# Which pairs of the expert layers use products of halves in the second layer

## The chip, the cores and the metric

The kernel runs on one core of a Trainium2 chip: one TensorE (PE, matrix products), VectorE (DVE), ScalarE (ACT), GpSimd (POOL), SyncE (SP, which issues transfers), one on-chip memory of 128 partitions, and PSUM, where PE's products collect. The metric is the device time of one execution in microseconds, the median of several executions.

## The reference

Causal attention with decay, then a dense mixture of four experts over all tokens, then a soft mixture of eight experts with four slots each. The change touches the middle part only:

```python
def _moe_ref(x, domain_probs, w1, w2):
    N, D = x.shape                       # 2304, 512
    E = w1.shape[0]                      # 4 experts, F = 1024
    p = domain_probs / (domain_probs.sum(-1, keepdims=True) + 1e-09)
    out = np.zeros((N, D), dtype=np.float32)
    for e in range(E):
        h = np.maximum(x @ w1[e], 0.0)
        out += p[:, e:e + 1] * (h @ w2[e])
    return out
```

## The kernel before, in words

**Numbers.** Every f32 operand is split into a high and a low f16 part, and each product is the sum of three f16 products: high by high, high by low, low by high. So each logical product of 128x128 weights is three matmuls.

**Tokens.** The 2304 tokens are 18 tiles of 128, six blocks of three tiles (384 columns, `NB`) and three pairs of blocks. Expert 0 runs beside the attention. Experts 1, 2 and 3 follow, pair after pair.

**Products of halves.** For a pair, x is cut in two by tokens and by inner dimension, w1 in two by two, and the four quarter results come from seven products instead of eight (Strassen's scheme in Winograd's form). It needs four sums of quarters of x (`x_sums`, line 696, a chain of 18 steps for one pair on GpSimd, VectorE and ScalarE), sums of quarters of w1, and additions of the products afterwards. There are two versions of the first layer:

- `quad` (matmuls at line 844, sums at 851, high and low parts at 855 and 858): only the first layer goes by halves. The second is `tile_l2`, whole: per tile of 128 tokens 24 matmuls of 128x512 (line 1105) and one weighted sum into the accumulator (line 658).
- `quad_sums` (matmuls 912, sums 929, 934, 987, copies 923, high parts 1400 or 1402, low parts 941 and 998): it also forms sums of quarters of h, because the second layer goes by halves too. That is `outputs`: seven products for each of three tiles, each of 12 matmuls of 128x256 (line 1041), each followed by one or two weighted sums (line 1053). It needs four sums T1 to T4 of quarters of w2 (`w2_sums`, lines 772, 781, 783).

Both versions have the row blocks m = 0 to 3 of a pair's hidden dimension, with seven products of six matmuls of 128x384 each. The operands of the second layer by halves carry the names "11", "12", "22" (quarters of h) and "1" to "4" (sums). `quad_sums` works in temporaries x, y, u and v of 384 columns. Three sets of them are used in turn. PSUM banks are `qA`, `qE`, `qF`.

**Which pair does what.** `PAIRS = (0, 3, 3, 2)` is the number of pairs of each expert by halves in the first layer, `PLAIN = (0, 1, 0, 0)` says that expert 1's pair 0 has a plain first layer (line 1075), and `OUT_H = (0, 0, 3, 2)` how many pairs go by halves in the second layer: none of expert 1, three of expert 2, two of expert 3.

**Memory.** Only one pair's x and sums have a home of their own in experts 2 and 3. All six blocks of x (`x_d`) and the sums of all pairs (`s_d`) are stored to DRAM once and loaded again ahead of each pair (`load_x`). The T sums of expert 3 are also staged in DRAM (`t_d`).

**Weights.** `prep_tasks` prepares an expert's weights: a maximum over the matrix (lines 496, 499, 503), spread over the partitions by a small PE matmul into `mp` (line 448), then a power of two as scale (lines 421 to 451), then high and low parts (541 and 544; 527 and 440 for w2) and sums of quarters (538).

**Order.** A planner, `Sched`, places each task on its engine at build time: a list scheduler with a cost per task and a key as priority, smallest first; some tasks may go to either of two engines. PE's own order is written out by hand (`in_order`). What the planner fixes is the instruction order of each engine; on the chip every engine follows its list and waits on semaphores.

## Time and profile before

| | |
|---|---|
| median of 3 runs | 971.86 us (971.3 to 973.75) |
| profiled execution | 969.51 us |
| its span in the trace | 967.8 us |
| mean granted clock of PE | 0.994 |
| PE busy | 929.4 us, 96% |
| VectorE busy | 674.9 us, 70% |
| ScalarE busy | 492.3 us, 51% |
| GpSimd busy | 423.3 us, 44% |
| chain that ended last | PE 75%, DVE 12%, DMA 3%, ACT 3% |

Busy times of PE overlap at their ends, so the distance between the starts of two runs of matmuls says more than a mean duration. Expert 1's plain layer begins near 357 us, its pair 1 at 417, pair 2 at 477, expert 2 at 535 (pairs 1 and 2 at 593 and 648), expert 3 at 703, and the second expert layer's matmuls at 914.

### The profile page before, as it was taken

Reading aid. Unit: us, or ns where it says so; the run is one execution under the profiler, and the core shown is the slowest. Engines: PE = TensorE matmul, PEld = TensorE weight load, DVE = VectorE, ACT = ScalarE, POOL = GpSimd, SP = SyncE. Lnnn points to the kernel's source line nnn. Section 1 sums busy time; section 2 is a strip of 40 time slices with the busy share of each in tenths; the row PEclk is TensorE's granted clock in tenths of the full one; section 3 lists DMA queues with packets and bytes.
Section 4 is the critical chain, followed back from the end, with each engine's and each line's share of the span. In section 5 each row is a group of like instructions: output and inputs, shape, how many; then the busy total and the mean of one; then the engine's idle time right before and its main releaser. Section 6 shows DMA issues by size and latency. Waiting matters only on the chain.

```text
span 967.8 us, 22183 instructions
## 1 busy us (share of the span) xinstructions
PE 929.4 (96%) x8984; PEld 627.1 (65%) x8984; DVE 674.9 (70%) x1295; ACT 492.3 (51%) x1094; POOL 423.3 (44%) x416
## 2 busy tenths in 40 slices
PE   7988999999999999999999999999999999999995
PEld 3567778787878865455454577686868768655331
DVE  7989987879776489747566687868987485433313
ACT  6878878878687465246143542616453250212123
POOL 3998786785654377731004340726553150000000
PEclk9999999999999999999999999999999999999998
DMA  8889999999999630643311344243433027913795
GB/s 227 187 171 169 187 184 197 195 192 163 202 177 224 120 121 25 258 182 124 111 65 44 123 163 151 76 143 121 164 101 132 1 76 238 348 70 122 239 359 195
DMA packets 270054, 153.50 MB, mean 159 GB/s; under 512 B 231776, under 2 KB 233824, under 8 KB 269952
## 3 DMA queue, kind: packets, MB, share of 16 engines
q1 hardware_dynamic: 269904, 152.02, 61.1%
q8 instruction: 70, 1.15, 0.5%
q14 instruction: 32, 0.26, 0.1%
q10 hardware_dynamic: 48, 0.07, 0.0%
HBM read 94.02 MB, written 16.25 MB: 114 GB/s over the span
## 4 chain that ended last, share of the span: by engine, by line
PE 75%; DVE 12%; DMA 3%; ACT 3%; issue 2%; POOL 2%; SPq 2%; DVEq 0%; ACTq 0%; POOLq 0%
PE pso L1105 10%; PE qA L912 7%; PE pso L612 6%; PE psh L591 6%; PE qA L1041 5%; PE qE L1041 4%; PE qE L912 4%; PE psh L634 3%; PE pso L652 3%; PE qF L1041 3%; PE s L1533 3%; PE qA L844 2%; PE pv L1622 2%; PE pso L1041 2%; PE qF L912 2%
## 5 line engine op out<-in xcount | busy, mean ns | idle before, releaser
L1041 PEld LDWEIGHTS <-arena 128*128 128x128 f16 x1260 | 123.1, 98 | 17.8 <-issue 1.8
L912 PEld LDWEIGHTS <-arena 128*128 128x128 f16 x840 | 82.0, 98 | 55.2 <-issue 3.5
L1402 POOL TENSOR_SCALAR arena<-arena 128x384 f16<-128x384 f32 (+5 forms) x75 | 56.8, 760 | 125.7 <-ACT arena L923 34.4
L591 PE MATMUL psh<-arena 128*128 128x128 f16 x1728 | 101.9, 219 | 0.0
L612 PE MATMUL pso<-arena 128*128 128x512 f16 x432 | 100.2, 382 | 0.0
L591 PEld LDWEIGHTS <-arena 128*128 128x128 f16 x1728 | 97.3, 98 | 0.4
L1105 PE MATMUL pso<-arena 128*128 128x512 f16 x432 | 95.0, 379 | 0.0
L1574 ACT ACTIVATE arena<-s,mx,qs 128x320 f32<-128x320 f32 (+4 forms) x144 | 91.6, 642 | 4.8 <-POOL arena L1591 1.8
L912 PE MATMUL qA<-arena 128*128 128x384 f16 x480 | 87.3, 326 | 0.7 <-DVE arena L929 0.3
L941 POOL TENSOR_TENSOR arena<-arena 128x384 f16<-128x384 f32 x64 | 63.9, 1008 | 46.6 <-ACT arena L1400 45.2
L1400 ACT ACTIVATE arena<-arena 128x384 f16<-128x384 f32 (+5 forms) x119 | 70.7, 605 | 26.8 <-DVE arena L934 18.0
L1591 POOL TENSOR_TENSOR arena<-arena 128x128 f16<-128x128 f32 (+4 forms) x79 | 69.6, 902 | 13.9 <-ACT arena L1400 12.0
L1105 PEld LDWEIGHTS <-arena 128*128 128x128 f16 x432 | 42.3, 98 | 49.8
L1554 DVE TENSOR_REDUCE mx<-s 128x1 f32<-128x576 f32 (+4 forms) x76 | 64.5, 850 | 8.9 <-PE s L1533 8.5
L612 PEld LDWEIGHTS <-arena 128*128 128x128 f16 x432 | 40.5, 99 | 44.1 <-issue 1.6
L1533 PE MATMUL s<-arena 128*128 128x128 f16 (+1 forms) x928 | 65.1, 212 | 4.1 <-ACT arena L1574 3.6
L696 POOL TENSOR_TENSOR arena<-arena 128x768 f32<-128x768 f32 (+2 forms) x25 | 51.4, 2061 | 30.1 <-DVE arena L696 24.8
L538 POOL TENSOR_TENSOR arena<-arena 128x512 f32<-128x512 f32 x23 | 35.1, 1531 | 61.7 <-DVE arena L544 56.4
L1533 PEld LDWEIGHTS <-arena 128*128 128x128 f16 x928 | 57.4, 98 | 6.7 <-issue 5.0
L1041 PE MATMUL qA<-arena 128*128 128x256 f16 x480 | 57.3, 273 | 0.0
L544 DVE SCALAR_TENSOR_TENSOR arena<-arena,wm 128x512 f16<-128x512 f32 x46 | 55.2, 1223 | 2.3 <-ACT arena L541 2.3
L1591 DVE TENSOR_TENSOR arena<-arena 128x64 f16<-128x64 f32 (+4 forms) x69 | 50.3, 767 | 7.1 <-POOL arena L1402 3.7
(275 smaller groups left out, 1860.2 us busy)
## 6 DMA issues: line engine op xcount, KB each, us to landing
arena<-in_moe_w_dram SPq DMA_DIRECT2D x66, 512.0 KB, 4.7
...
arena<-xd SPq DMA_DIRECT2D x10, 768.0 KB, 4.3
arena<-in_moe_w_dram SPq DMA_DIRECT2D x9, 768.0 KB, 9.6
...
xd<-arena SPq DMA_DIRECT2D x6, 768.0 KB, 7.1
...
```

What stands on the lines that cost most here:

```text
L591: nc.tensor.matmul(out=ps[:, m, :], lhsT=wt["w1" + a, 0][:, kk, ms], rhs=xT[j][:, b + kk, ts], start=(n == 0), stop=(n == 3 * KD - 1))
L612: nc.tensor.matmul(out=ops[u], lhsT=a[:, m, ts], rhs=wt["w2" + b, 0][:, m, :], start=(m == 0 and z == 0), stop=(m == KF - 1 and z == 2))
L912: nc.tensor.matmul(out=ps[c], lhsT=wS[e][o][:, w, k, ms], rhs=a[z][:, k], start=(first and i == 0), stop=(i == 5), skip_group_check=True)
L941: h_t[q][m] = y = T(LO, {"DVE": 0.55, "Pool": 1.0}, -30, lambda eng: by[eng].tensor_tensor(out=l_, in0=a, in1=h_, op=ALU.subtract), [y], r ...
L1041: nc.tensor.matmul(out=ps[c, t], lhsT=hq[a][x][:, m, ts], rhs=wq[y][:, m, :], start=(first and m == 0 and n == 0), stop=(m == KF // 2 - 1 ...
L1105: nc.tensor.matmul(out=cell[0], lhsT=a[:, m, ts], rhs=wt["w2" + b, e][:, m, :], start=(len(left) == KF - 1 and z == 0), stop=(not left and ...
L1400: nc.scalar.activation(out=out, in_=x, func=AF.Copy, scale=scale)
L1402: nc.gpsimd.tensor_scalar(out=out, in0=x, scalar1=scale, scalar2=0.0, op0=ALU.mult, op1=ALU.add)
L1533: nc.tensor.matmul(out=o, lhsT=qT[u][:, 2 * h + w, :], rhs=kT[kk][:, 2 * h + w, k0:k0 + n_], start=(w == 0), stop=(w == 1 and mask is None))
L1554: nc.vector.tensor_reduce(out=mx[:, 0:nh].rearrange("p (a h) -> p a h", a=sv.shape[1]), in_=sv, axis=AX.X, op=ALU.max, negate=True)
L1574: nc.scalar.activation(out=P[:, x], in_=sv[:, x // hb, x % hb], func=AF.Exp, scale=qs[u][:, 4:5], bias=mxs[n][:, 4 + x:5 + x], accum_out=s ...
L1591: by[eng].tensor_tensor(out=t[:, :, d0:d0 + n_], in0=P[:, :, s0:s0 + n_], in1=t[:, :, s0:s0 + n_], op=ALU.subtract)
```

## The change

- **Pairs.** `OUT_H` now names pairs: 1 and 2 of expert 1, 0 and 1 of expert 2, 0 and 1 of expert 3. `ORDER` gives the order of pairs: expert 2 begins with pair 2, which goes by halves in the first layer only (`quad` and `tile_l2`), then pairs 0 and 1 in both. Expert 1's pairs 1 and 2 use `quad_sums` and `outputs`.
- **Sums of w2 for expert 1** (`w2_sums(1)`) are new, beside the sums of x; expert 2's follow its w1 preparation; expert 3's T sums stay on the chip, so `t_d`, its stores and its loads are gone.
- **x and its sums.** The home of x is now pair 2's pages (`HOME = 2`). Sums of x are made for pair 1, pair 0, then (behind the sums of w2) pair 2; before it was pair 1, pair 2, pair 0. The pages of blocks 0, 1 and 3 become operands of the second layer ("11", "22", "12") once their x is stored. Expert 1's pair 1 has its own place for "12" (`hq_own`), in the scratch pages of pair 2's sums. `hq_free` makes the writers of those operands wait for stores and sums.
- **Temporaries.** y, u and v have two sets, and x has three places.
- **Scale steps.** The small steps between the maximum and the scale (`A[4]` to `A[6]`) have the key -35 instead of that of their expert. On PE the spread `mp` for expert 1's w2 stands after 24 matmuls of the plain first layer instead of after 72.
- **Weights by operand.** A product waits for its own weights (`w1_of`) and not for all of the matrix.
- **Expert 3's plain last pair** loads one quarter of w1 again, with one ScalarE and one VectorE instruction.
- **End.** Other pages come free at other moments; 89 pages of the second expert layer's weights are loaded ahead of its first matmul, 92 before.

On the whole program PE has 252 more matmuls of 128x256 (1512, 1260 before) and 144 fewer of 128x512 at `tile_l2` (288, 432 before); its other groups keep their counts.

```diff
-OUT_H = (0, 0, 3, 2)
+ORDER = ((), (0, 1, 2), (2, 0, 1), (0, 1))
+OUT_H = ((), (1, 2), (0, 1), (0, 1))
...
+        def w1_of(o):
+
+            if len(w1_t) != 37:
+                return w1_t
+            i = (1, 5, 7, 17, 12, 16, 14)[o]
+            return [w1_t[1 + i], w1_t[19 + i]]
...
-                return in_order(0.98, go, list(deps) + w1_t + s_t[p],
+                return in_order(0.98, go, list(deps) + w1_of(o) + s_t[p],
...
-            x, y, u, v = tmp
+            x = [tmps[0][0], tmps[1][0], third.get((e, p), third[None])][three]
+            y, u, v = tmps[two][1:4]
             X, Y, U = (lambda a=a: a for a in (x, y, u))
-            old, now = free_at[m % len(tmps)], {}
-            free_at[m % len(tmps)] = now
+            wait = hq_free.get((e, p), {})
+            old = {**free_at[two], "4": x_free[three]}
+            free_at[two] = now = {}
...
-        for p in range(PAIRS[e]):
+        for p in ORDER[e]:
             h_t = [{}, {}]
             before = None
-            if p < OUT_H[e]:
+            if p in OUT_H[e]:
...
+    SMALL = -35
...
-        t = T("DVE", 0.1, key, A[4], ta)
-        t = A[5](key, [t])
-        sc_t = T("DVE", 0.5, key, A[6], [t])
+        t = T("DVE", 0.1, SMALL, A[4], ta)
+        t = A[5](SMALL, [t])
+        sc_t = T("DVE", 0.5, SMALL, A[6], [t])
...
-        for p, tmp in ((1, (p_S[0][0], p_S[0][1])), (2, (p_S[0][0], p_S[0][1])), (0, (wA, wA + 2))):
-            x_halves(p, p_S[p])
-            y = y + {1: [], 2: w2_1, 0: e0_t + w1_1}[p]
-            s_t[p] = y = steps(56 + p % 3, x_sums(p, lambda tmp=tmp: [page(x, 2)[:, 0:2 * NB] for x in tmp]), X_COST, y)
+        sums_of_x(1, 56, (p_T[2], p_T[1]), [])
+        sums_of_x(0, 57, (wA + 6, wA + 14), s_t[1] + e0_t + w1_1)
...
+        sums_1, last = w2_sums(1, ams["w2", 1], [raw2 + 2 * i for i in range(4)], w2_end, 57.5, in_place(1, s_t[1] + w1_1))
+        sums_of_x(2, 58, (wA + 6, wA + 14), s_t[0] + last[0])
...
+        for q, p in (("11", xT_page[0]), ("22", xT_page[1]), ("12", xT_page[3]), ("1", hT_p), ("2", hT_p + 3), ("3", wA + 8),
                      ("4", wA + 11)):
...
+        hq_own[1, 1] = {"12": h_of(wA + 4)}
+        hq_free[1, 1] = {"11": kept_x[0], "22": kept_x[1], "12": kept_s[0] + s_t[2]}
+        hq_free[1, 2] = {"12": kept_x[3], "4": kept_x[2]}
...
+        w1_2, last = prep_tasks(2, 0, R, last, [end_s1[-1]], 60, ([p0_, p0_ + 2], [end_s1[0]] + kept_s[1]))
+        last = sums_of_2(last[0:2], (0, 1), 60, w1_2)
```

Three places show how the order moves. In the changed kernel most lines stand 1 to 40 further down: L696 becomes L697, L851 L869, L912 L932, L929 L949, L941 L962, L987 L1012, L1053 L1082, L544 L545, L658 L659, L772 L782.

VectorE where expert 1's pair 1 begins, before (L658 is a tile sum of pair 0's second layer, L696 a step of the sums of x, L851 and L858 are `quad`'s sums and low parts):

```order
L658 SCALAR_TENSOR_TENSOR arena<-pso,pw,arena 128x512
L696 TENSOR_TENSOR arena<-arena 128x768
L658 SCALAR_TENSOR_TENSOR arena<-pso,pw,arena 128x512
L851 TENSOR_TENSOR qF<-qF,arena 128x384
L696 TENSOR_TENSOR arena<-arena 128x768
L858 SCALAR_TENSOR_TENSOR arena<-qF,arena 128x384
L658 SCALAR_TENSOR_TENSOR arena<-pso,pw,arena 128x512
L851 TENSOR_TENSOR arena<-qA,arena 128x384
```

and changed, the same place (L949 and L962 are `quad_sums`' sums and low parts):

```order
L659 SCALAR_TENSOR_TENSOR arena<-pso,pw,arena 128x512
L697 TENSOR_TENSOR arena<-arena 128x768 x4
L659 SCALAR_TENSOR_TENSOR arena<-pso,pw,arena 128x512
L697 TENSOR_TENSOR arena<-arena 128x768 x3
L949 TENSOR_TENSOR qF<-qF,arena 128x384
L697 TENSOR_TENSOR arena<-arena 128x768 x2
L962 TENSOR_TENSOR arena<-arena 128x384
L949 TENSOR_TENSOR arena<-qA,arena 128x384
L659 SCALAR_TENSOR_TENSOR arena<-pso,pw,arena 128x512
```

Before, one step of the sums of x stands behind the pair's first sum `qF`; changed, two stand behind it, seven more with one tile sum between them just ahead, and they belong to pair 2's chain instead of pair 0's.

GpSimd from the end of the weight preparation to expert 1's pairs, before (L538 and L772 are sums of quarters of w1 and w2, L1402 and L941 high and low parts of expert 2's h):

```order
L696 TENSOR_TENSOR arena<-arena 128x768
L538 TENSOR_TENSOR arena<-arena 128x512 x2
L696 TENSOR_TENSOR arena<-arena 128x768 x21
L772 TENSOR_TENSOR arena<-arena 128x2x256 x3
L538 TENSOR_TENSOR arena<-arena 128x512 x8
L1402 TENSOR_SCALAR arena<-arena 128x384 x2
L941 TENSOR_TENSOR arena<-arena 128x384
```

and changed (L1012 is a sum, L1435 a high part of expert 1's h):

```order
L782 TENSOR_TENSOR arena<-arena 128x2x256
L697 TENSOR_TENSOR arena<-arena 128x768
L782 TENSOR_TENSOR arena<-arena 128x2x256 x3
L697 TENSOR_TENSOR arena<-arena 128x768
L782 TENSOR_TENSOR arena<-arena 128x2x256
L697 TENSOR_TENSOR arena<-arena 128x768 x14
L1012 TENSOR_TENSOR arena<-arena 128x384
L1435 TENSOR_SCALAR arena<-arena 128x384
```

Before, the next work of GpSimd behind the sums of x is expert 2's w2 and w1; changed, sums of expert 1's w2 lie between the sums of x, and expert 1's sums of h follow the last fourteen at once.

VectorE at the end of expert 1's pair 2, where expert 2's w1 is prepared, before (L544 is a low part of w1):

```order
L544 SCALAR_TENSOR_TENSOR arena<-arena,wm_6736 128x512 x2
L658 SCALAR_TENSOR_TENSOR arena<-pso,pw,arena 128x512
L544 SCALAR_TENSOR_TENSOR arena<-arena,wm_6736 128x512 x4
L658 SCALAR_TENSOR_TENSOR arena<-pso,pw,arena 128x512
L544 SCALAR_TENSOR_TENSOR arena<-arena,wm_6736 128x512
L929 TENSOR_TENSOR qF<-qF,arena 128x384
L941 TENSOR_TENSOR arena<-arena 128x384
```

and changed (L1082 is an output sum of a product of halves, L869 the first sum of expert 2's `quad`):

```order
L545 SCALAR_TENSOR_TENSOR arena<-arena,wm_6728 128x512 x2
L1082 SCALAR_TENSOR_TENSOR arena<-qF,pw,arena 128x256
L1082 SCALAR_TENSOR_TENSOR arena<-qE,pw,arena 128x256
L545 SCALAR_TENSOR_TENSOR arena<-arena,wm_6728 128x512
L1082 SCALAR_TENSOR_TENSOR arena<-qA,pw,arena 128x256
L545 SCALAR_TENSOR_TENSOR arena<-arena,wm_6728 128x512
L1082 SCALAR_TENSOR_TENSOR arena<-qE,pw,arena 128x256
L545 SCALAR_TENSOR_TENSOR arena<-arena,wm_6728 128x512
L869 TENSOR_TENSOR qF<-qF,arena 128x384
```

Before, the low parts of w1 lie between tile sums of 128x512; changed, between output sums of 128x256, which come more often. Fourteen L545 and fourteen L1082 stand in the stretch whose end is shown.

## Rows read from the trace of the kernel before

**Rows 1.** The page, section 1: engine, busy us (share of the span), instructions.

```profile
PE 929.4 (96%) x8984; PEld 627.1 (65%) x8984; DVE 674.9 (70%) x1295; ACT 492.3 (51%) x1094; POOL 423.3 (44%) x416
```

**Rows 2.** Windows: length, busy us (instructions) by engine, granted clock, DMA share, GB/s.

```profile
380.00:418.00 38.00, 38.00 (x196) 19.06 (x195) 30.65 (x32) 11.46 (x18) 27.50 (x14) 1.00 0.48 190
418.00:477.00 59.00, 58.74 (x315) 30.67 (x313) 35.55 (x59) 27.28 (x49) 7.22 (x5) 1.00 0.42 142
477.00:535.00 58.00, 58.00 (x313) 30.45 (x312) 36.76 (x57) 21.93 (x41) 12.63 (x8) 1.00 0.19 61
535.00:593.00 58.00, 58.00 (x425) 41.53 (x424) 43.90 (x81) 25.29 (x48) 18.29 (x23) 1.00 0.47 151
...
648.00:703.00 55.00, 54.95 (x421) 40.92 (x419) 48.74 (x84) 28.50 (x55) 32.81 (x31) 1.00 0.38 131
920.00:940.00 20.00, 19.40 (x174) 6.36 (x176) 4.32 (x22) 4.89 (x10) 0.00 (x0) 1.00 1.05 397
```

**Rows 3.** PE's waits over the span: total us, times, longest us.

```profile
PE mp L448 <- DVE wm L503: 2.9, 2, 2.2
...
PE qF L1041 <- DVE arena L1053: 0.6, 1, 0.6
...
PE qA L1075 <- DVE arena L1086: 0.2, 1, 0.2
```

**Rows 4.** PE's timeline, expert 1 pair 0's second layer: start us, length, instruction.

```profile
420.32 4.05 PE L1105 MATMUL pso<-arena 128*128 128x512 f16 x18
424.21 1.14 PE L844 MATMUL qA<-arena 128*128 128x384 f16 x6
```

**Rows 5.** PE's timeline, products of an expert 2 pair's second layer.

```profile
640.32 1.47 PE L1041 MATMUL qF<-arena 128*128 128x256 f16 x12
641.63 1.47 PE L1041 MATMUL qE<-arena 128*128 128x256 f16 x12
```

**Rows 6.** VectorE by line and form, 357 to 825: count | busy us, mean ns | idle before.

```profile
L544 DVE SCALAR_TENSOR_TENSOR arena<-arena,wm 128x512 f16<-128x512 f32 x39 | 45.5, 1188 | 0.7 <-ACT arena L541 0.7
L941 DVE TENSOR_TENSOR arena<-arena 128x384 f16<-128x384 f32 x36 | 26.0, 735 | 6.1 <-POOL arena L1402 4.3 <-ACT arena L1400 1.6
L934 DVE SCALAR_TENSOR_TENSOR arena<-qA,arena 128x384 f32<-128x384 f32 x40 | 21.8, 548 | 1.6 <-PE qA L912 1.6
L1053 DVE SCALAR_TENSOR_TENSOR arena<-qA,pw,arena 128x256 f32<-128x256 f32 x40 | 18.8, 475 | 12.6 <-PE qA L1041 12.4
...
L987 DVE TENSOR_TENSOR arena<-arena 128x384 f32<-128x384 f32 x18 | 15.1, 841 | 0.7
...
L658 DVE SCALAR_TENSOR_TENSOR arena<-pso,pw,arena 128x512 f32<-128x512 f32 x18 | 13.4, 747 | 19.5 <-PE pso L1105 19.5
...
L858 DVE SCALAR_TENSOR_TENSOR arena<-qA,arena 128x384 f16<-128x384 f32 x8 | 4.5, 558 | 6.4 <-ACT arena L855 6.3
```

**Rows 7.** GpSimd's timeline, steps of the sums of x.

```profile
387.72 14.41 POOL L696 TENSOR_TENSOR arena<-arena 128x768 f32<-128x768 f32 x7 [1.44 <-DVE arena L696]
```

**Rows 8.** The page, section 6: stores of x, KB each, us from issue to landing.

```profile
xd<-arena SPq DMA_DIRECT2D x6, 768.0 KB, 7.1
```

**Rows 9.** VectorE's timeline while GpSimd works on the sums of x.

```profile
359.38 2.13 DVE L538 TENSOR_TENSOR arena<-arena 128x512 f32<-128x512 f32 x1
361.44 3.44 DVE L544 SCALAR_TENSOR_TENSOR arena<-arena,wm 128x512 f16<-128x512 f32 x2
...
365.73 3.26 DVE L544 SCALAR_TENSOR_TENSOR arena<-arena,wm 128x512 f16<-128x512 f32 x2
```

**Rows 10.** ScalarE's timeline, expert 2 pair 1: writes of the temporary `u`.

```profile
605.13 0.48 ACT L923 ACTIVATE arena<-qF 128x384 f32<-128x384 f32 x1
...
619.01 0.48 ACT L923 ACTIVATE arena<-qF 128x384 f32<-128x384 f32 x1
```

**Rows 11.** VectorE's timeline, the last low part of that pair.

```profile
629.88 1.62 DVE L941 TENSOR_TENSOR arena<-arena 128x384 f16<-128x384 f32 x1
```

**Rows 12.** VectorE's timeline while GpSimd is idle.

```profile
536.21 0.73 DVE L544 SCALAR_TENSOR_TENSOR arena<-arena,wm 128x512 f16<-128x512 f32 x1
```

More of the change, by code (lines that the diff above doesn't have):

```diff
@@ L786, in w2_sums, with halves_tasks @@
                 out[i].append(then(y))
-            last = [ends, ends]
+            last = [ends, ends] if len(all_bufs) < 4 else [*before, *([ends] if c == 0 else [])]
+            done += ends
+        if len(all_bufs) == 4:
+            last = [done, done]
         return out, last
-    carry = []
-    def halves_tasks(e, w1_t, w2_t, s_t, tmps, between=lambda j: [], used_up=None, plain_t=None, next_x=None, t_sums=None,
-                     t_used=None):
+    carry, hq_own, hq_free, prod, third_at = [], {}, {}, {}, {}
+    def halves_tasks(e, w1_t, w2_t, s_t, tmps, between=lambda j: [], used_up=None, plain_t=None, next_x=None, t_sums=None):
         T = sc.task
@@ L1030, in go @@
                 def go():
-                    calm[0] = (e, p, i, t) != (2, 0, 4, TPB - 1)
+                    calm[0] = i < 4 or t < TPB - 1 or (e, then.get((e, p))) not in TENSE
                     if first:
@@ L1219, in halves_tasks, with prep_tasks @@
         return end_s, end, todo
-    def prep_tasks(e, ti, bufs, before, there, key, more=None, mid=None):
+    SMALL = -35
+    def prep_tasks(e, ti, bufs, before, there, key, more=None, mid=None, there_lo=()):
         T = sc.task
@@ L1254, in prep_tasks @@
                     bufs, us = bufs + more[0], (2, 3)
-                    last += [there + more[1]] * 2
+                    last += [more[1]] * 2
                 if n < 4:
@@ L2063, in moe_attention_kernel @@
         kept_s = {p: [T("DMA", 1.0, 90, lambda p=p, i=i: nc.sync.dma_start(out=s_d[p][i], in_=s_place(p, i)), [s_t[p][-1], *s_t[p]])
-                      for i in range(4)] for p in s_t}
-        xR[:] = [xT[0], xT[1], xS[0]]
+                      for i in range(4)] for p in range(len(s_d))}
+        HOME = 2
+        for e, p in ((1, 1), (None, HOME)):
+            xR[(e, p) if e else None] = [xT[2 * p], xT[2 * p + 1], xS[p]]
         def load_x(p, deps, sums=True):
-            out = [T("DMA", 2.0, 30 + x, lambda x=x: nc.sync.dma_start(out=page(xT_page[x], 3), in_=x_d[2 * p + x]),
-                     deps + kept_x[2 * p + x] + kept_x[x] + kept_s[0]) for x in range(2)]
+            out = [T("DMA", 2.0, 30 + x, lambda x=x: nc.sync.dma_start(out=page(xT_page[2 * HOME + x], 3), in_=x_d[2 * p + x]),
+                     deps + kept_x[2 * p + x] + kept_x[2 * HOME + x]) for x in range(2)]
@@ L2071, in load_x, with h_of @@
             if sums:
-                out += [T("DMA", 1.0, 32 + i, lambda i=i: nc.sync.dma_start(out=s_place(0, i), in_=s_d[p][i]), deps + kept_s[p] + kept_s[0])
+                out += [T("DMA", 1.0, 32 + i, lambda i=i: nc.sync.dma_start(out=s_place(HOME, i), in_=s_d[p][i]), deps + kept_s[p])
                         for i in range(4)]
             return out
-        for q, p in (("11", xT_page[3]), ("22", xT_page[4]), ("12", raw2 + 2), ("1", hT_p), ("2", hT_p + 3), ("3", wA + 8),
+        def h_of(p):
+            v = page(p, 3, F16).rearrange("p (z m c) -> p z m c", z=2, c=NB)
+            return [v[:, z] for z in range(2)]
@@ new lines, in moe_attention_kernel, with sums_of_2 @@
+        w2_2, last = prep_tasks(2, 1, R, [last[0], s_t[2]], s_t[2] + kept_s[0], 59,
+                                there_lo=[prod[1, 1, 2, t] for t in range(TPB)] + [third_at[1, 1]])
+        sums_2 = {f"T{i + 1}": [] for i in range(4)}
+        def sums_of_2(last, cs, key, late=[]):
+            y, last = w2_sums(2, ams["w2", 2], R, [w2_2 + x for x in last], key,
+                              in_place(2, [end_s1[0]] + kept_s[1] + kept_x[2] + late), cs)
+            for b, z in named(y).items():
+                sums_2[b] += z
+            return last
@@ L2117, in moe_attention_kernel @@
-        sc.gate = None
-        w2_3, last = prep_tasks(3, 1, R, last, end_1, 60)
-        held_st = {0: [], 1: []}
-        def staged(i, c):
-            x = i // 2
-            v = page(st_pages[x], 1, F16).rearrange("p (z n) -> p z n", z=2)
-            def then(y):
-                y = T("DMA", 0.8, 60, lambda: nc.sync.dma_start(out=t_d[i][:, :, c, :], in_=v), [y])
-                held_st[x] = [y]
-                store_3[i].append(y)
-                return y
-            return (*(v[:, z].rearrange("p (k n) -> p k n", k=2) for z in range(2)),
-                    held_st[x] + [end_s1[-1]] + kept_x[2] + kept_s[2], then)
+            i = ORDER[2].index(p) + 1
@@ L2136, in sums_of_3 @@
-            for x in spent:
-                load_sum(*x)
+            y, last = w2_sums(3, ams["w2", 3], R, [w2_3 + x for x in last], 60.5, in_place(3, end_1))
+            sums_3.update(named(y))
             sc.gate = None
@@ L2349, in used_up @@
         def used_up(p):
+            if p == 0:
+                dyn.free(p0_, 6)
             if p == PAIRS[e] - 1:
-                for x in p_S[0]:
-                    dyn.free(x, 2)
+                dyn.free(raw2, 6)
             fill(0)
@@ L2365, in moe_attention_kernel @@
             dyn.free(p, 3)
-        for x in range(2):
-            xT_page[NBLK - 2 + x], xT[NBLK - 2 + x] = xT_page[x], xT[x]
+        mg = page(dyn.alloc(1))
         side += rest
```

189 lines of the change are left out of this document (103 added, 86 removed).

## The prediction, made before the changed kernel ran

> **What bounds the kernel now.** I read the page first, then the waits of PE, then windows of one token pair each, then PE's and VectorE's timelines at the places the change touches.
>
> PE is busy 929.4 of 967.8 us [rows 1]. In the windows of expert 1's pairs 1 and 2 and of expert 2's first pair, the ones that change, PE is busy 58.74 of 59, 58.00 of 58 and 58.00 of 58 us, at a granted clock of 1.00, the 2.4 GHz level [rows 2]. So here the end of the kernel moves with the time that PE's own matmuls take, as long as nobody makes PE wait. Little does now: the largest wait of PE on VectorE in the expert stage is 2.2 us at the spread of a scale (`mp`), five more are 0.6 down to 0.2 us, 1.6 in all [rows 3]. VectorE is the next engine: 35.55 and 36.76 us in the windows of expert 1's pairs 1 and 2, 43.90 of 58 and 48.74 of 55 us in expert 2's first and third [rows 2]. The last is 0.89, and PE still lost only 0.05 us there. That is the heaviest load of which the trace shows that it is carried.
>
> **PE, the term that decides.** A pair's second layer, whole, is 6 tiles of 24 matmuls of 128x512, 144 in all; by products of halves it is 7 products of 3 tiles of 12 matmuls of 128x256, 252. Durations in the by-line view overlap, so the price is the distance between starts. Eighteen matmuls of 128x512 run from 420.32 to 424.21, 0.216 us each [rows 4]; twelve of 128x256 from 640.32 to 641.63, 0.109 us each [rows 5]. A pair whole is 144 x 0.216 = 31.1 us, by halves 252 x 0.109 = 27.5 us: 3.6 less. Expert 1's pairs 1 and 2 go over (-7.2), expert 2's first pair comes back (+3.6). First layers keep their 168 matmuls of 128x384 in either form. The sum on PE is **-3.6 us**. All other matmul groups keep their counts.
>
> A rule of the Trainium skill speaks against this ("TensorE: Matmul & The Clock Gate", section "Back-to-back issue gap"): in a stream of weight loads and matmuls it gives about 81 ns a matmul at 128 columns and 131 ns at 512. By a straight line between them 256 columns would take an estimated 98 ns, and the change would cost 252 x 0.098 - 144 x 0.131 = +5.8 us. The rows show 0.216 and 0.109, nearly the ratio of the columns, and agree with that section's other formula, its gap for one isolated matmul.
>
> **VectorE, and what hides it.** A pair with first layer by halves only takes 28 instructions of about 0.55 us (sums out of PSUM and low parts, L851, L858) and 6 tile sums of 0.747 us: 15.4 + 4.5 = 20 us. Halves in both layers takes, per row block m of four, nine sums and low parts (L929, L934, L998) at 0.55, one L987 at 0.841 and about two of the five low parts L941 at 0.735 (36 of 100 fell to VectorE), and 21 output sums of 0.475: 4 x 7.1 + 10.0 = 38 us [rows 6]. So VectorE gains 18 us in each of expert 1's pairs, 36 in both. The weight sums of expert 2 (about 9 us) leave this stretch for expert 2's first pair. 35.55 + 36.76 + 36 - 9 = 99 us stand against PE's 117 - 7.2 = 110 us: 0.90, as heavy as the 0.89 that is carried now. On average there is cover; bunches decide. If the cover fails, each microsecond over costs one. ScalarE and GpSimd take their parts of the same sums; they had 27.28 and 7.22 of 59 us there [rows 2], and are far from full.
>
> *Start of expert 1's pair 1.* Today the sums of x for pair 2, then pair 0, come ahead. Changed, pair 2's chain is last and still runs when pair 1 starts: GpSimd has fourteen sums L697 in a row ahead of its first sum of h, and VectorE's first sum `qF` (L949) stands among L697s. GpSimd needs 14.41 us for 7, 2.06 each [rows 7], and the chain also goes through VectorE and ScalarE. A chain of 18 steps, some eight of them on GpSimd and the rest on VectorE (about 1 us) and ScalarE, is 18 to 20 us. Pair 0's starts near 393, once the expert's first layer has its weights and their scratch pages are free, and ends near 413; pair 2's ends near 431. Its scratch is wanted for the high part of "12" by PE's clock near 434. Pair 0's x is stored from about 413 and lands near 420 with 7.1 us for such a store [rows 8]; its pages are wanted for "11" near 424. The spare is some 3 us. Lower end 0; upper end: two chains a fifth longer are 7 to 8 us, less 3 of spare, some 4 us. I take 0.3, nearer to zero, because the same chain now delays no matmul in 380 to 418 (PE 38.00 of 38) [rows 2].
>
> *Expert 1 to expert 2.* Fourteen L545 (expert 2's weights; L544 of before) now lie between fourteen output sums. At 0.73 [rows 12] to 1.63 us (half of the pair at 365.73 [rows 9]) plus 14 x 0.48 that is 17 to 30 us; PE meanwhile has 14 products of 1.31 and 18 matmuls of 128x384 at one and a half times 0.109 us, 21 us. By the mean 1.188 [rows 6] it is 23; where VectorE has no gap its instructions overlap by 0.08 (359.38 + 2.13 against 361.44 [rows 9] shows 0.07), 2 us in 28, so 21. Zero to 7; I take 0.5, since the mean just fits.
>
> *The spread `mp`.* It stood after 72 matmuls of expert 1's plain layer, now after 24, with its maximum L504 ahead of one more L545. PE would reach it near 361.2; L538 ends at 361.5 and an L544 near 363.2 [rows 9], so `mp` starts near 363.4: 2.2 us, what it waits today [rows 3]. Change 0; ends -2.2 (the L538 is not in the way) and +1.7 (a second L544 is).
>
> *Two sets of temporaries instead of three.* ScalarE writes `u` from qF at 605.13 and 619.01, with one between [rows 10], 6.9 us apart, so a set comes round after 13.9 us instead of 20.8. One of the two longest lives of the twenty is from 619.01 to the end of L941 at 631.50, 12.5 us [rows 10, 11]. It fits by 1.4 us: 0, and the rival below is the other end.
>
> *End of the kernel.* Three pages fewer are free ahead of the second expert layer, 3 x 256 KB at 397 GB/s = 2.0 us of transfer in a stretch whose DMA share is 1.05; PE is nevertheless busy 19.40 of 20 us there [rows 2], so the stream is not late by much. 0 to 2.0; I take 0.2.
>
> *Everything else at nothing.* The staging of T sums in DRAM goes (8 stores, 4 loads); expert 3's extra quarter of w1 is one load, one ScalarE and one VectorE instruction during pairs on which PE has 55 us. The five small waits of [rows 3], 1.6 us, may go or stay: -1.6 to 0, I take 0.
>
> **Sum**: -3.6 + 0.3 + 0.5 + 0 + 0 + 0.2 = -2.6 us on the profiled 969.51 us. The median is 971.86, 2.35 higher; the same difference gives **969.3 us**. A measurement here tells about 0.3%, 2.9 us, so the forecast lies just on the edge between faster and same.
>
> **Rivals.**
> 1. *Nothing is given back* and some old small waits go: -3.6 to -5.2, 966.7 to 968.3, say 967.9. For it: VectorE's 0.89 carried without loss. Against it: three places with little spare.
> 2. *VectorE becomes the bound at expert 1's pair 1*, or at the change to expert 2: 2.2 to 6 us given back, 970.5 to 974.8, middle 971.7. For it: beside GpSimd's L696 the two L544 at 365.73 took 3.26 us, 1.6 each, against 0.73 at 536.21 [rows 9, 12], and the new order has GpSimd busy on sums just when VectorE's new work begins. The Trainium skill ("GPSIMD Engine Reference", section "Key points") says that the two share SBUF interfaces and that VectorE instructions with two SBUF inputs contend; these rows agree, though what of the doubling is this cause they do not show. Against: L934 out of PSUM holds 0.55 as its mean [rows 6].
> 3. *Slower: two sets are too few.* Where the last L941 of a block ends over 13.9 us after its `u`, the next block's write waits, qF is not given back, and PE stops. All 20 blocks now use two sets. It turns slower than before at 2.6 us, 0.13 us a block, so at a life of 14.0 us, and by over 0.3% at 14.2, 1.7 more than the one above; at 14.25, 20 x 0.35 - 2.6 = +4.4, 976.3 us. For it: expert 1's GpSimd is more loaded than expert 2's. Against: eighteen of twenty lives were shorter than the one of the rows.
> 4. *Half-width matmuls cost more than their columns.* By the by-line means (273 against 379 ns) 252 x 0.273 - 144 x 0.379 = +14.2, 986 us. The distances of starts [rows 4, 5] are against it; they hold whole stretches.
>
> That the change does not do what it says is out: the changed order has 252 more matmuls of 128x256 and 144 fewer of 128x512.
>
> **How the numbers follow.** Forecast as it stands, 968.3 to 970.5: 0.45. Rival 1: 0.20. Rival 2: 0.20. Rival 3: 0.12. Rival 4: 0.03. The bound of 0.3% is at 968.95: somewhat under half of the forecast's case and all of rival 1 is faster, 0.40; the rest of it and rival 2 are same, 0.45; rivals 3 and 4 slower, 0.15. The range leaves out rivals 3 and 4 and a little at each edge: 967.0 to 974.0.
>
> **What would show it.** Right: in the windows of expert 1's pairs PE stays as good as full and pair 1's first output product starts some 55 us after the pair's start instead of 59; products of 128x256 start every 1.31 us; PE's waits in the expert stage sum to no more than some 5 us. Rival 2: gaps of PE at the first `qA`, `qF` of expert 1's pair 1, or at expert 2's first, released by VectorE, GpSimd or a store of x. Rival 3: small gaps every 6.9 us, released by ScalarE's L923 line. Wrong in the first term: another distance of starts. Later waits in the second expert layer, by DMA, would show the page count.

## The result: slower by 1.1%, and the profile after

The changed kernel takes 982.79 us (median of six, 979.36 to 987.17), the kernel before beside it 971.94 us. The ratio is 1.0109, 95% interval 1.0083 to 1.0135. The forecast of 969.3 us, with a range up to 974.0, was wrong, and by its sign. The profiled execution took 983.19 us with a span of 981.5 us, 13.7 us more than [rows 1]'s 967.8.

Section 1 of the page after (engine, busy us and share, instructions):

```profile
PE 932.5 (95%) x9092; PEld 640.1 (65%) x9092; DVE 703.4 (72%) x1333; ACT 503.3 (51%) x1114; POOL 452.1 (46%) x443
```

PE's busy time grew by 3 us although its work shrank. VectorE is busy 28 us longer over the whole span. What changed are PE's waits in the expert stage (total us, times, longest us), of which [rows 3] had 2.9 us and five of 0.6 or less:

```profile
PE qE L932 <- DVE arena L954: 3.7, 2, 2.5
...
PE mp L449 <- DVE wm L504: 2.6, 2, 2.0
PE qA L932 <- ACT arena L943: 2.5, 2, 2.2
PE qA L932 <- DVE arena L949: 2.5, 3, 2.0
PE pso L653 <- DVE arena L644: 2.4, 1, 2.4
```

To see all that PE lost, I took PE's timeline from 355 us to the second expert layer's first matmul and subtracted, for each run of matmuls, their number times the distance of starts ([rows 4, 5]; 0.163 us for 128x384) from the time to the next run. Before, 5.0 us are lost in that way, after 20.5. Less the 3.6 us that PE saves that is +11.9; the plain layer of expert 1 begins 1.1 us later, and some 0.7 us come at the end. Together it is the 13.7 us. Four places make up the loss: the start of expert 1's pair 1 (6.6 us), two waits for bank qE (5.6), the spread `mp` (3.6, before 2.4) and a wait in expert 3's plain pair (2.5).

**Place 1, expert 1's pair 1.** PE's timeline (start us, length, instruction):

```profile
431.14 2.11 PE L932 MATMUL qA<-arena 128*128 128x384 f16 x12 [2.22 <-ACT arena L943]
435.24 1.18 PE L932 MATMUL qA<-arena 128*128 128x384 f16 x6 [1.99 <-DVE arena L949]
436.22 2.12 PE L932 MATMUL qF<-arena 128*128 128x384 f16 x6
438.14 1.87 PE L932 MATMUL qE<-arena 128*128 128x384 f16 x6
```

Two waits, 2.2 and 2.0 us, and behind them six matmuls that take 1.92 us (436.22 to 438.14) instead of 0.98. The windows of the same place (length, busy us by engine, granted clock, DMA share, GB/s) show why: in 434 to 436 PE was busy 0.76 of 2 us, and in the next 4 us the granted clock is 0.55 and 0.60 in the mean, so mostly at the 1.2 GHz level. In 400 to 440 VectorE is busy 36.5 of 40 us.

```profile
400.00:420.00 20.00, 20.00 (x95) 9.09 (x93) 19.75 (x16) 3.37 (x4) 13.15 (x7) 1.00 0.08 26
420.00:440.00 20.00, 15.79 (x78) 8.07 (x77) 16.73 (x18) 6.61 (x12) 12.14 (x7) 0.91 0.40 160
434.00:436.00 2.00, 0.76 (x5) 0.48 (x5) 2.00 (x4) 0.78 (x2) 0.30 (x1) 1.00 0.00 0
436.00:438.00 2.00, 2.00 (x9) 0.98 (x7) 1.25 (x3) 1.37 (x3) 1.07 (x1) 0.55 0.00 0
438.00:440.00 2.00, 2.00 (x9) 0.93 (x7) 1.49 (x3) 0.00 (x0) 1.02 (x2) 0.60 0.10 24
```

Before the change VectorE was busy 24.2 us in the same two windows:

```profile
400.00:420.00 20.00, 20.00 (x98) 9.42 (x97) 13.34 (x15) 3.87 (x5) 12.83 (x7) 1.00 0.38 157
420.00:440.00 20.00, 20.00 (x118) 11.43 (x116) 10.86 (x23) 13.63 (x26) 0.96 (x1) 1.00 0.61 226
```

ScalarE, VectorE and GpSimd there, after the change:

```profile
429.49 0.84 ACT L700 ACTIVATE arena<-arena 128x768 f16<-128x768 f32 x1 [2.14 <-POOL arena L697]
430.24 0.47 ACT L943 ACTIVATE arena<-qF 128x384 f32<-128x384 f32 x1
430.61 0.48 ACT L943 ACTIVATE arena<-qA 128x384 f32<-128x384 f32 x1
```

```profile
405.76 0.95 DVE L697 TENSOR_TENSOR arena<-arena 128x768 f32<-128x768 f32 x1
...
408.98 2.39 DVE L697 TENSOR_TENSOR arena<-arena 128x768 f16<-128x768 f32 x1
...
428.34 4.46 DVE L697 TENSOR_TENSOR arena<-arena 128x768 f32<-128x768 f16 x2
432.73 1.99 DVE L962 TENSOR_TENSOR arena<-arena 128x384 f16<-128x384 f32 x1
434.64 0.55 DVE L949 TENSOR_TENSOR arena<-qA,arena 128x384 f32<-128x384 f32 x1
```

```profile
427.16 2.29 POOL L697 TENSOR_TENSOR arena<-arena 128x768 f32<-128x768 f32 x1 [1.07 <-DVE arena L697]
430.35 3.95 POOL L697 TENSOR_TENSOR arena<-arena 128x768 f32<-128x768 f32 x2 [0.89 <-DVE arena L697]
436.93 1.64 POOL L697 TENSOR_TENSOR arena<-arena 128x768 f16<-128x768 f32 x1 [2.63 <-ACT arena L700]
```

ScalarE's copies out of qF and qA (L943), for which PE waits, stand behind L700, a step of pair 2's sums of x that waits for GpSimd's L697. VectorE then takes 4.46 us for two L697, and L949, for which PE waits next, stands behind them. The chain's last GpSimd step ends at 438.6, where the forecast had 431. One L697 on VectorE takes 0.95 us at 405.76, where GpSimd waits, and 2.39 at 408.98, beside a GpSimd L697. The low parts of expert 1's sums of w2 (L793) stand among them and take 1.76 to 2.12 us beside GpSimd.

**Place 2, bank qE.** PE's and VectorE's timelines in expert 2's second pair:

```profile
622.84 1.14 PE L932 MATMUL qF<-arena 128*128 128x384 f16 x6
626.49 1.28 PE L932 MATMUL qE<-arena 128*128 128x384 f16 x6 [2.51 <-DVE arena L954]
```

```profile
620.36 0.15 DVE L504 TENSOR_REDUCE wm<-wm 128x1 f32<-128x4 f32 x1
...
621.49 0.28 DVE L452 TENSOR_REDUCE wm<-mp 128x1 f32<-128x128 f32 x1
...
624.02 0.57 DVE L949 TENSOR_TENSOR qF<-qF,arena 128x384 f32<-128x384 f32 x1 [0.46 <-PE qF L932]
...
624.96 0.55 DVE L1024 SCALAR_TENSOR_TENSOR arena<-qE,arena 128x384 f16<-128x384 f32 x1
...
625.89 0.55 DVE L954 SCALAR_TENSOR_TENSOR arena<-qE,arena 128x384 f32<-128x384 f32 x1
```

PE waits for L954 at 625.89, which gives bank qE back. It stands behind L949, which needs PE's run into qF that ended at 624.0. ScalarE's high part had been there since 621.0, so L1024 and that L954 could have run before; the planner put the steps of a scale (L504, L452 and the others) and L949 ahead, although those small steps take less than 1 us together. A wait of the same kind costs 1.2 us at 502.7: there L1024 stands ahead of L949, but the L954 that gives qE back stands behind it, and no step of a scale stands between 496 and 504. Behind the second wait the clock is down again (six matmuls in 1.92 us; granted clock 0.50 in 628 to 630).

**Place 3, expert 3's plain pair.** PE, VectorE and SyncE's queue:

```profile
855.81 5.13 PE L653 MATMUL pso<-arena 128*128 128x512 f16 x23
863.30 0.39 PE L653 MATMUL pso<-arena 128*128 128x512 f16 x1 [2.37 <-DVE arena L644]
```

```profile
861.90 0.35 DVE L2361 TENSOR_SCALAR arena<-arena 128x192 f16<-128x192 f32 x1 [6.43 <-DMA arena<-arena]
...
862.70 0.55 DVE L644 SCALAR_TENSOR_TENSOR arena<-psh,arena 128x384 f16<-128x384 f32 x1
```

```profile
831.83 19.42 SPq L2245 DMA_DIRECT2D arena<-in_moe_w_dram  x18
851.74 12.25 SPq L2365 DMA_TRANSPOSE arena<-arena  x2
```

L2361 rewrites a buffer that a transposing DMA of the routing weights reads. That DMA stands behind 18 loads, 39 pages, of the second layer's weights. L2361 waits 6.43 us for it, L644 waits behind L2361, and PE for L644.

The queue itself is not new. Before the change 18 loads stood ahead of the same two transposes too (L2336 there, and L2332 for L2361):

```profile
802.63 34.27 SPq L2215 DMA_DIRECT2D arena<-in_moe_w_dram  x18
837.24 10.92 SPq L2336 DMA_TRANSPOSE arena<-arena  x2
```

```profile
846.07 0.35 DVE L2332 TENSOR_SCALAR arena<-arena 128x192 f16<-128x192 f32 x1 [1.23 <-DMA arena<-arena]
```

But three of them began at 802.6 to 803.8 and the other fifteen from 819.9 on, so that the first transpose was issued 12.2 us after the plain pair's start at 825.0. Changed, all 18 begin from 831.8 on, and it is issued 16.1 us after the pair's start at 835.6. The wait of L2332 was 1.23 us and did not reach PE.

### The profile page after: what moved, and what is told of

Read it like the earlier page. It is cut to its first block, busy times and chain, and to the rows that moved or that the text cites. A ratio compares the mean times of both kernels' runs of the same rounds, so it can differ in the third digit from the quotient of the medians.

```text
span 981.5 us, 22522 instructions
## 1 busy us (share of the span) xinstructions
PE 932.5 (95%) x9092; PEld 640.1 (65%) x9092; DVE 703.4 (72%) x1333; ACT 503.3 (51%) x1114; POOL 452.1 (46%) x443
## 4 chain that ended last, share of the span: by engine, by line
PE 71%; DVE 15%; issue 4%; POOL 4%; DMA 2%; ACT 2%; SPq 1%; DVEq 0%; POOLq 0%; ACTq 0%
PE qA L932 9%; PE psh L592 7%; PE pso L613 7%; PE qA L1071 6%; PE qE L932 5%; PE qE L1071 4%; PE pso L1134 3%; PE s L1566 3%; PE qF L1071 3%; PE psh L635 3%; PE pso L653 3%; PE pv L1655 2%; PE qF L932 2%; PE pso L1071 2%; DVE arena L545 2%
## 5 line engine op out<-in xcount | busy, mean ns | idle before, releaser
L932 PEld LDWEIGHTS <-arena 128*128 128x128 f16 x1008 | 99.5, 99 | 76.8 <-issue 15.7
L1435 POOL TENSOR_SCALAR arena<-arena 128x384 f16<-128x384 f32 (+5 forms) x78 | 57.5, 740 | 161.6 <-ACT arena L943 101.5
L932 PE MATMUL qA<-arena 128*128 128x384 f16 x576 | 105.7, 328 | 5.2 <-ACT arena L943 2.5
L962 POOL TENSOR_TENSOR arena<-arena 128x384 f16<-128x384 f32 x77 | 78.2, 1027 | 69.9 <-ACT arena L1433 68.3
L613 PE MATMUL pso<-arena 128*128 128x512 f16 x432 | 100.6, 384 | 0.0
L1433 ACT ACTIVATE arena<-arena 128x384 f16<-128x384 f32 (+5 forms) x136 | 79.3, 594 | 28.5 <-DVE arena L954 20.6
L697 POOL TENSOR_TENSOR arena<-arena 128x768 f32<-128x768 f32 (+2 forms) x26 | 52.6, 2024 | 37.6 <-DVE arena L697 30.0
L1071 PE MATMUL qA<-arena 128*128 128x256 f16 x576 | 68.8, 273 | 0.0
L1134 PE MATMUL pso<-arena 128*128 128x512 f16 x288 | 63.5, 379 | 0.0
L932 PE MATMUL qE<-arena 128*128 128x384 f16 x288 | 55.2, 332 | 3.7 <-DVE arena L954 3.7
L1071 PE MATMUL qE<-arena 128*128 128x256 f16 x432 | 53.1, 273 | 0.0
```

The source lines that it names most:

```text
L613: nc.tensor.matmul(out=ops[u], lhsT=a[:, m, ts], rhs=wt["w2" + b, 0][:, m, :], start=(m == 0 and z == 0), stop=(m == KF - 1 and z == 2))
L932: nc.tensor.matmul(out=ps[c], lhsT=wS[e][o][:, w, k, ms], rhs=a[z][:, k], start=(first and i == 0), stop=(i == 5), skip_group_check=True)
L962: h_t[q][m] = y = T(LO, {"DVE": 0.55, "Pool": 1.0}, -30, lambda eng: by[eng].tensor_tensor(out=l_, in0=a, in1=h_, op=ALU.subtract), [y], r ...
L1071: nc.tensor.matmul(out=ps[c, t], lhsT=hq[a][x][:, m, ts], rhs=wq[y][:, m, :], start=(first and m == 0 and n == 0), stop=(m == KF // 2 - 1 ...
L1134: nc.tensor.matmul(out=cell[0], lhsT=a[:, m, ts], rhs=wt["w2" + b, e][:, m, :], start=(len(left) == KF - 1 and z == 0), stop=(not left and ...
L1433: nc.scalar.activation(out=out, in_=x, func=AF.Copy, scale=scale)
```

## Experiments

Each ratio is to the kernel before on the same chip.

**Undo one part: the key of the small steps.**

```diff
-        t = T("DVE", 0.1, SMALL, A[4], ta)
-        t = A[5](SMALL, [t])
-        sc_t = T("DVE", 0.5, SMALL, A[6], [t])
+        t = T("DVE", 0.1, key, A[4], ta)
+        t = A[5](key, [t])
+        sc_t = T("DVE", 0.5, key, A[6], [t])
```

> The changed kernel with one part undone: the small steps between an expert's maximum and its scale have the key of their expert again instead of -35, so they come behind the sums of h. Theory 'order' (the small steps push L1024 behind the next block's sum at 626): the 2.5 us wait for qE there goes, 2.5 to 4 us less; the spread of expert 1's scale goes back behind more matmuls, and its wait is 2 to 2.3 us as before. Rival: the waits at 502 and 626 come from the lowest key of L1024 alone; both stay and the time is the changed kernel's within 1 us.

Ratio 1.0055 (1.0038 to 1.0072), 976.74 us. Both waits for qE are gone (in the profiled execution, at 974.25 us the shortest of eight). VectorE at the place that answers to 624, where L1024 and the L954 for qE now stand ahead of L949 and of L504:

```profile
618.15 0.54 DVE L1024 SCALAR_TENSOR_TENSOR arena<-qE,arena 128x384 f16<-128x384 f32 x1
...
619.75 0.54 DVE L954 SCALAR_TENSOR_TENSOR arena<-qE,arena 128x384 f32<-128x384 f32 x1
...
620.68 0.55 DVE L949 TENSOR_TENSOR qF<-qF,arena 128x384 f32<-128x384 f32 x1
...
621.62 0.14 DVE L504 TENSOR_REDUCE wm<-wm 128x1 f32<-128x4 f32 x1
```

**The other way to mend that order: an early high part of "12".**

```diff
-                z = T("Act", 0.5, -30, ... AF.Relu),
+                z = T("Act", 0.5, -41, ... AF.Relu),
...
-                h_t["12"][m] = t["l12"] = T("DVE", 0.56, -30, ...
+                h_t["12"][m] = t["l12"] = T("DVE", 0.56, -41, ...
```

> The changed kernel, but the two steps that lead to giving back bank qE (the high part of "12" on ScalarE and its low part on VectorE, L1022 and L1024) get the planner's highest priority (key -41) instead of the lowest of their block (-30). Theory 'order': PE's waits for qE at 502.7 and 626.5 us (1.2 and 2.5 us, the second followed by 1.6 us at the lower clock) come from L1024 being listed behind the next block's sum out of qF, which itself waits for PE. They go, about 5.5 us of 982.8: 977. Rival 'load': VectorE has too much to do there whatever the order; the waits appear again nearby and the time stays within 1.5 us of 982.8.

Ratio 1.0115 (1.0090 to 1.0140): nothing gained. Both waits for qE went, but seven of 0.3 to 0.8 us came in other blocks. The plain pair of expert 3 began only 1.9 us earlier, and the wait before L653 grew to 3.9 us, so that this gain was lost there. The cause of the two waits stands; this mending does not pay.

**The queue of place 3.** The first attempt freed three pages later:

> The changed kernel, but only three instead of six pages come free for the second layer's weights at the end of expert 3's pair 1; the other three a stage later. Theory 'queue': the transposing DMA of the routing weights stands behind eighteen page loads in the queue where it stood behind fifteen; the next block's VectorE step L2361 waits for it until 861.9, L644 behind it, and PE 2.4 us. With fifteen loads the gap goes: 2 to 2.5 us less, about 980.5. Rival 'bandwidth': the DMA engines are full anyway, the transpose lands as late and the gap stays; 982.8.

Ratio 1.0140 (1.0125 to 1.0155). The edit missed its aim: there were still 18 loads ahead of the transposes, and the wait was 4.4 us. The second held 16 pages back:

```diff
         side += rest
-        fill(0)
+        fill(16)
```

> The changed kernel; only the order of loads on SyncE's queue is different: 16 of the 39 pages of second-layer weights that are loaded at the start of expert 3's plain pair stay back until the transposing DMA of the routing weights has been issued (23 pages ahead of it instead of 39). The previous run with fewer freed pages did not shorten that burst (42 pages) and its gap grew to 4.4 us, so 'queue' is still open against 'bandwidth'. Theory 'queue': the transposes wait behind 10 MB of loads that start only when expert 3's pair 1 is done; with 6 MB they land 10 us earlier, L2361 does not wait, and PE's gap before L653 (2.4 us in the changed kernel, up to 4.4 in the others) is gone: 2.4 to 4 us less, 979 to 980.5. Rival 'bandwidth' or 'later stream': the 16 pages come back as a wait at the second layer's matmuls, and the time stays at 982.8.

Ratio 1.0065 (1.0044 to 1.0086), 978.13 us. SyncE and PE:

```profile
830.55 9.83 SPq L2245 DMA_DIRECT2D arena<-in_moe_w_dram  x12
840.70 2.71 SPq L2365 DMA_TRANSPOSE arena<-arena  x1
```

```profile
854.54 5.34 PE L653 MATMUL pso<-arena 128*128 128x512 f16 x24
```

The transpose for which L2361 waited is issued at 840.70, behind 23 pages, and PE's 24 matmuls run through. From the start of the plain pair to the first matmul of the second expert layer it is 88.9 us, as before the change (91.4 in the changed kernel): the later stream of pages costs nothing there. These 2.5 us are what the run shows for place 3. The other 2 us by which its profile is shorter lie ahead of the plain pair and behind that first matmul.

**Both mended.**

> The changed kernel with both orders mended that the runs so far showed: small steps with their expert's key (as e6), and 16 pages held back behind the transposing DMA (as e5). Theory 'parts add up': of e6's waits the one before L653 (1.5 us) goes too, the rest stays, mostly 5.4 us at expert 1's pair 1: 1.5 to 2.5 us below e6, ratio to the kernel before 1.003 to 1.004, some 974.5 us. Rival: the held-back pages return as a wait in the second layer, ratio as e6's 1.0055.

Ratio 1.0022 (1.0012 to 1.0032), 972.54 us. So mending the two orders takes 0.87 of the 1.09% away; in this profile the slow clock behind `mp` and behind pair 1's waits is gone too. What is left beyond the kernel before is mainly 5.4 us at expert 1's pair 1: the same two waits (2.2 and 2.0 us) and some small ones.

**Whether pair 1's own second-layer form is the load.** Expert 1's pair 1 with its second layer whole (`OUT_H = ((), (2,), (0, 1), (0, 1))`; a wait of expert 2's w2 preparation for that pair's products goes with it):

> The changed kernel with one part undone: expert 1's pair 1 goes by halves in the first layer only, its second layer whole; pair 2 of expert 1 and all other pairs as changed. PE has 3.6 us more of work. Theory 'late sums of x': the waits at the start of pair 1 (2.2 and 2.0 us, 1.7 us of slow clock, 0.6 of the rest) come from pair 2's sums of x running into the sums of h of pair 1. With plain sums of h they shrink to below 1.5 us: 982.8 + 3.6 - 5.5 = 981. Rival 'load': the waits are from too much work on VectorE in all of expert 1; they move to pair 2, 985 to 987. Rival 'two sets of temporaries': nothing of the waits changes, 986.

Ratio 1.0093 (1.0076 to 1.0110), 979.8 us. PE's loss at that start is 2.2 instead of 6.6 us, so about two thirds of it hang on that pair's sums of h. The time itself says little: PE has 3.6 us more to do, and the wait of place 3 is 4.05 us here.

**Other orders for the sums of x.** First the planner's price for VectorE beside GpSimd, `SHARED` (0.8, 0.62) to (0.7, 0.45), without and with the early high part, both with the pages held back:

> As e5 (pages held back), and the planner is told another price for VectorE beside GpSimd when both read two operands from the on-chip memory: speed 0.45 instead of 0.62 (0.7 instead of 0.8 with one), which is nearer to 0.73 against 1.6 us in the trace. The whole order is planned anew. Theory 'late sums of x by a wrong price': the sums of x of pair 2 and the steps that wait for them are placed so that PE's waits at expert 1's pair 1 (7 us with the slow clock in the runs so far) shrink to 2 us or less, and the others too; 972 to 976. Rival 'load': VectorE and GpSimd have too much to do before 435 us whatever the order; PE waits there 5 us or more, and the time is 979 or above.

> As e7, and the two steps that lead to giving back bank qE with the highest key (as in the first run). Theory: with the other order and the new price both kinds of waits of PE in the expert stage are down to the single steps of 0.3 to 0.5 us: 970 to 975. Rival: the gain of one order is lost to another, and the time is within 1.5 us of e7's.

Ratios 1.0174 (1.0150 to 1.0199) and 1.0132 (1.0102 to 1.0161). PE waits 3.5 us at 431 and 4.5 at 448. Then e9's kernel with the chain begun at block 0, 1 or 2 of pair 1, and with scratch pages on which nothing of pair 1 waits (the edit is shown in part):

```diff
-        sums_of_x(2, 58, (wA + 6, wA + 14), s_t[0] + last[0])
+        chain_go = sc.handle()
+        sums_of_x(2, 58, (raw2 + 6, wA + 14), s_t[0] + last[0] + [chain_go])
+        opens[1, 1, 0] = chain_go
```

> As e9; in addition pair 2's sums of x may begin only when PE issues the second product of expert 1's pair 1 (block 0), and use scratch pages on which nothing of pair 1 waits. The same work, later. Theory 'late sums of x': PE's waits at pair 1's start come from VectorE and ScalarE being stuck behind the chain's steps; with the chain begun later they are less, but block 0 still meets it: 2 to 4 us less than e9. Rival 'load': the waits only move into pair 1; the time is e9's or above.

> As e10, but the sums of x of pair 2 begin with block 1. Theory 'late sums of x': the first block's sums of h have VectorE for themselves, the 5.4 us at pair 1's start go, and the saving of 3.6 us on PE shows at last: ratio 0.997 to 0.999, 968.5 to 970.5 us. Rival 'load': about 16 us of GpSimd and 14 of VectorE must still fit beside pair 1; PE waits 3 us or more somewhere in pair 1, and the ratio is 1.001 or above.

> As e11, with block 2. Theory 'late sums of x': like e11 within 1 us, since the sums of pair 2 are wanted only some 40 us later. Rival 'load': the chain now runs beside the output sums and pair 2's beginning waits for it: 2 us or more above e11.

Ratios 1.0102 (1.0087 to 1.0117), 1.0121 (1.0106 to 1.0136), 1.0287 (1.0270 to 1.0305). The waits move and grow. Block 0, PE and VectorE:

```profile
443.57 2.08 PE L934 MATMUL qE<-arena 128*128 128x384 f16 x6 [5.08 <-DVE arena L956]
```

```profile
437.29 3.90 DVE L956 SCALAR_TENSOR_TENSOR arena<-arena 128x384 f32<-128x384 f32 x2
441.11 0.55 DVE L951 TENSOR_TENSOR qF<-qF,arena 128x384 f32<-128x384 f32 x1
```

PE's first wait now comes 11 us later than in e9 and is 5.1 us. Two sums (L956, both operands on chip) take 3.90 us beside the chain, and qE's L956 comes behind them. A wait of 2.5 us for qE at 503.9, with its slow clock behind it, adds some 4 us that are not of pair 1's start. With blocks 1 and 2, expert 2's weights are late too (waits of up to 3.2 and 4.5 us for L545). None of these orders gives cover; what the rival 'load' said came true in e7 and in e10 to e12. Forcing the chain to begin earlier was not tried.

**Taking the helpers' time away, order kept** (on e9's kernel; part of the edit for the sums of x; the one for the sums of w2 is alike). These kernels leave out nearly all of those sums: an addition works on 24 of 384 or 16 of 256 columns, and a low part is only set to zero. They tell what the sums' time costs and are no kernels to use.

```diff
+            if p == 2 and o[-1] == "l":
+                return (LO, lambda eng: by[eng].memset(at_(o), 0.0), deps)
+            if p == 2:
+                return (LO, lambda eng: by[eng].tensor_tensor(out=at_(o)[:, :, 0:24], ...
```

> As e9, every engine's order kept, but the VectorE and GpSimd steps of pair 2's sums of x work on 24 of 384 columns or only write zeros (the sums of pair 2 are left out; what is computed for that pair is wrong in part). Theory 'late sums of x': PE's waits at the start of expert 1's pair 1 (2.4, 2.1, 0.5 and 0.4 us in e9) go nearly all: 5 us less, ratio to the kernel before 0.997. Rival 'sums of w2': they shrink by less than 2 us, since the low parts of expert 1's sums of w2 fill VectorE as much; ratio 1.000 to 1.002.

> As e9, order kept, but expert 1's sums of w2 work on 16 of 256 columns and their low parts only write zeros (the sums of w2 of expert 1 are left out). Theory 'late sums of x': pair 2's chain starts earlier on the chip, since its pages come free earlier and VectorE is less busy; the waits of PE shrink by 2 to 5 us, ratio 0.997 to 1.000. Rival: the chain itself is the slow part and the waits stay, ratio 1.002.

> As e9, order kept, both sums light (left out as in e13 and e14). Shows what is left of PE's waits in expert 1 when nothing beside the expert's own pairs is in the way, and so whether the term of 3.6 us stands: theory, waits in the expert stage as in the kernel before (2.3 us at the spread of the scale and little else) and ratio 0.995 to 0.997. Rival 'half-width matmuls cost more in the long run' or 'two sets of temporaries': ratio 1.000 or above even so.

Ratios 0.9974 (0.9961 to 0.9987), 0.9988 (0.9978 to 0.9998) and 0.9977 (0.9966 to 0.9988). PE in e13, at the place of the two waits:

```profile
428.45 3.09 PE L937 MATMUL qA<-arena 128*128 128x384 f16 x18
...
437.70 1.14 PE L937 MATMUL qA<-arena 128*128 128x384 f16 x6 [0.32 <-DVE arena L954]
```

The waits at the start are gone but for 0.3 us, although VectorE is still busy 19.3 of 20 us in 400 to 420; in 420 to 440 it is 11.6 us, 17.1 in e9. Without the sums of w2 alone, one wait of 1.6 us stays there. With both light, PE's waits on VectorE at L504 and in expert 1 to 3's sums are

```profile
PE mp L449 <- DVE wm L504: 2.3, 1, 2.3
...
PE qA L941 <- DVE arena L958: 1.1, 4, 0.3
```

and the plain pair of expert 3 begins at 822.9 instead of 825.0 us, 465.5 us behind the start of expert 1's plain layer instead of 467.7. PE's waits on this way sum to 4.7 us, 3.8 before. A gain of 2.3 us in spite of 0.9 us more of waits accounts for 3.2 of the 3.6 us.

**The same PE work on other pairs.** All of expert 2's pairs by halves, first beside the change as it is (seven pairs), then instead of expert 1's pair 1 (six, on e9's kernel):

> The changed kernel with expert 2's first pair by halves in both layers too (seven pairs by halves instead of six). It has 252 more matmuls of 128x256 and 144 fewer of 128x512. Theory of the sum: PE's part is worth 3.6 us a pair; if expert 2's first pair has cover on VectorE, 979.2. Rival 'load': VectorE, which prepares expert 2's sums of w2 there, cannot carry it; PE waits 4 us or more and the time is 983 or above. Rival 'half-width matmuls cost more than their columns': +14 us.

> As e9, but six pairs by halves in another split: of expert 1 only pair 2 in both layers, of expert 2 all three (expert 1's pair 1 whole in the second layer). PE has the same work as in the changed kernel. Theory 'load beside expert 1's pair 1': its waits there shrink from 5.4 to 2.2 us as in e3; expert 2's first pair takes some back, as in e4 (up to 4 us); ratio 1.000 to 1.003. Rival: e4's waits in expert 2 were from the small steps, which have their old place here; then ratio 0.998 or less.

Ratios 1.0134 (1.0118 to 1.0151) and 1.0069 (1.0051 to 1.0087). In expert 2's first pair PE then waits 1.0, 0.3 and 1.7 us for L949, L954 and L793. In the second run the wait of 2.5 us for qE is back, with L1024 behind L949 again and no scale's steps beside it: the small steps were what brought that order about in the changed kernel, but not the only thing that can.

## Why the prediction was wrong, step by step

PE's timeline in the changed kernel, products of expert 1's pair 2, one of the two pairs that went over:

```profile
524.57 1.47 PE L1071 MATMUL qE<-arena 128*128 128x256 f16 x12
525.88 1.47 PE L1071 MATMUL qF<-arena 128*128 128x256 f16 x12
```

- **PE's term, -3.6 us: right.** The distance of the two starts above is 1.31 us, 0.109 us a matmul, as in [rows 5], and e15 shows most of the term in the time (0.9977; 3.2 of 3.6 us accounted for). Rival 4 falls. The figures of the Trainium skill ("TensorE: Matmul & The Clock Gate", section "Back-to-back issue gap") for a stream of weight loads and matmuls, by which the change would have cost PE an estimated 5.8 us, do not hold here either.
- **Start of expert 1's pair 1: 0.3 taken, 4 at most; 6.6 measured, 5.4 in e9.** The step that failed is the cover. The mean load was about right: 99 us were forecast for expert 1's two pairs, and VectorE was busy about 103 in 420 to 540. But the load of 0.9 was compared with a pair of expert 2 beside which expert 3's weights are prepared and no chain of sums of x runs. Here the sums of w2 and two chains of sums of x come just ahead. VectorE's load in the 40 us of the place, 36.5 of 40 or 0.91, is hardly above the 0.89 that was carried; what differs is what the steps for which PE waits stand behind. The forecast counted when the chain's *pages* are wanted and found 3 us to spare; PE did not wait for pages but for ScalarE's and VectorE's steps queued behind the chain. That is rival 2's mechanism, a little past its upper end of 6 us (which gives 974.3 us by its own sum, not 974.8), and it was given 0.20.
- **"Everything else at nothing": 5.6 us.** The new key of the small steps was priced only where it moves `mp`. That it also changes VectorE's order in pairs far from `mp` was left out, although the key is named among the changes.
- **End of the kernel: 0.2 taken, 2.5 measured, by another way.** The forecast priced the count of pages and not the moment at which they come free. Before, the loads ahead of the transposes began while expert 3's pair 1 still ran; now they begin only near its end, and counted from the plain pair's start the first transpose is issued 4 us later. From the second layer's first matmul on it is 54.4 us, 53.9 before, so that the count itself cost 0.5 at most.
- **Waits counted at their own length.** Behind three waits of 2.0 to 2.5 us (`mp`, the second of pair 1 and the second for qE) the granted clock fell to about 0.5, at 1.4 to 1.7 us extra each. The wait of 2.2 us in [rows 3] had shown none.
- **Right:** the wait of `mp` itself (2.2 taken, 2.04), and two sets of temporaries: no wait of PE is traced to them (by its releaser, ScalarE waited once for a set, 0.4 us, in e6, e9 and e13), and rival 3, the one on the slower side, is not how it became slower.
- **Right by luck:** the handover to expert 2 (0.5 taken, 0.6 measured). The forecast had VectorE's fourteen L545 in mind; PE's wait of 0.47 us there ends with a ScalarE copy (L885) that stands behind two steps of expert 2's sums of w2 (L791).

What stays open is how much of place 1 is the slower rate of VectorE beside GpSimd and how much plain work: taking away either helper's time removes most of the wait. Open too is why the clock fell behind some waits only.
